# Attention into a SwiGLU feed-forward on one core: a wait ahead of later q loads, a last tile in three pieces, and a sum of squares as six products

## The chip, the cores and the metric

The kernel runs on one core of one Trainium2 chip. The metric is the device time of one execution in microseconds (us). Beside the times there is one profiled execution, taken by the hardware profiler, from which all views of the profile come. The names of the engines in the profile: PE is TensorE (its matmuls), PEld the weight loads of TensorE, which overlap PE, DVE is VectorE, ACT is ScalarE, POOL is GpSimd, SP is SyncE. An engine's name with a q behind it (SPq, POOLq) stands for its sequencer, which issues DMAs and waits on semaphores.

## The reference

Attention with a squared relu in the place of the softmax, and behind it an RMS norm and a feed-forward of SwiGLU form. The sizes are 8 batches, 12 heads, 448 positions, 64 columns to a head; 768 columns in the model, 1536 in the feed-forward.

```
scores = (1 / sqrt(64)) * (q @ k.T)             # per batch and head: 448 x 448
attn   = max(scores, 0) ** 2 / 448
x      = (attn @ v), heads side by side         # 3584 x 768
rms    = sqrt(mean(x * x, axis=-1) + 1e-6)
xn     = x / rms * rms_g
g      = xn @ w_gate                            # 768 -> 1536
val    = xn @ w_val
out    = (g * sigmoid(g) * val) @ w_out         # 1536 -> 768
```

All inputs and the output are float32; the kernel computes its products in bf16 with float32 accumulation.

## The kernel before

**Layout.** Everything is held transposed: x and xn have the model's columns on the partitions (6 blocks of 128) and the batch's 448 positions along the free axis; the hidden layer (hT) has 12 blocks of 128. A product with 128 rows of weights is split into two halves of the array, of 64 rows each (and, in the projections, 64 columns), which run beside each other: in the profile such a matmul is "64*64 64x448". Output tiles have 128 positions on the partitions; two batches (896 positions) make seven tiles. Tile 3 of each pair crosses the border of its batches.

**One batch's work.** q, k and v come from memory with a cast to bf16. Scores for two heads at a time (`scores_full`, L462) go to PSUM, from there through a relu into an r tile (L450, on ACT or DVE) and are squared in place (L454). `attend` (L562) multiplies them with v and evicts x to SBUF (L625). Then x's squares are summed: L635 squares in float32, L637 accumulates over pairs of blocks, `close` (L641) adds the last two, and a product with a matrix of ones (`norm_sums`, L856) sums over the partitions and spreads the result. `norm_scale` (L663) makes rstd by Ln and Exp on ACT and scales x to xn on DVE (L678). The feed-forward (`ffn`, L978) then has 24 projection groups, gate and value in turns (silu at L870, hidden product at L884), and, for each output tile, an out-projection (`outproj`, L911) in two groups of 384 columns with 24 half-array products each. `store` (L933) copies a group from PSUM to an output tile in SBUF (L941 on ACT, L939 on DVE); when both halves are there, `send` (L954) issues the tile's DMAs on SP (L964), one for each run of rows that lie together in memory.

**Batch 0 and the head.** Batch 0 is done in two halves of 224 positions so that the first products can start early. For its first half the squares are in bf16 (L629), and class `Sums` (L832) sums them with ones-products of the full array, two blocks at a time (L848). The second half is summed as every other batch is. Batches 0 and 1 are loaded in large pieces and transposed on PE (PE_T is 2). While the planner sees PE idle for more than 0.3 us in the head, it writes matmuls whose result nobody reads (`fill`, L1051) into the order.

**Later batches' loads.** Batches 2 to 7 are loaded in another form, with heads and columns side by side: q in one DMA of 112 x 4 x 768 elements, k in seven (L300), v in two (L286), all issued by POOL. SP then issues eight DMA transposes (`transpose_dma`, L314, L324) for a batch, four for k and four for q, which turn the loaded pieces into the operands of the scores. A load of batch b+2 may start when the buffer of batch b has been read: for q and k when batch b has been turned, for v when its last attention products are done.

**What sets the order.** The pools keep no order of their own: the whole order is written at build time by a planner (class Planner, L62 to L164), a small simulation of the five engines. Every `Op` has a cost for each engine that may run it, things that it depends on (`deps`), a rank, and for scores and attention a `due` condition, which asks how far the feed-forward of an earlier batch has come (`past`, L990, on the notes ("gv", fraction) and ("o", fraction) that a group carries). The planner always takes the engine whose next step can begin first, and lets the op write its instructions. The order on the chip is then fixed for each engine's queue, and semaphores between them follow from the data. `Stream` (L697) holds the feed-forward's groups and, in steps, emits one product of one group on the upper half of the array and one of another on the lower (`Group.emit`, L796, L802: nearly all matmuls of the feed-forward carry this one line). A DMA's landing time in the plan is estimated by `arrives` (L245): a fixed time, and kilobytes by a rate, one DMA after another. The main loop (from L1073) adds the work of batch b+2 (loads, transposes, attention) together with the feed-forward of batch b.

## Time and profile before

| what | us |
|---|---|
| three runs | 454.03, 454.59, 456.85; median 454.59 |
| the profiled execution | 453.62 |
| its span in the profile | 451.9 |
| PE busy | 440.2 |
| DVE, ACT, POOL busy | 241.7, 268.8, 76.8 |
| POOL busy with the 42 issues of k pieces (L300) | 33.1 |
| mean clock of TensorE over the span | 0.993 of full |

The span is the time from the first to the last record; 1.7 us of the profiled execution lie around it. A group's line in the profile has its source line, engine, operation, the tiles written and read, the number of partitions and elements, a count, then busy time and mean, and last the idle time of the engine just ahead of it with what ended it ("<-issue": nothing that the profile shows). In a timeline each row begins with its start in us from the span's start and its length. A row of a table by windows has the stretch, its length, then for PE, PEld, DVE, ACT and POOL the busy time with the number of instructions in brackets, then the mean clock that TensorE was granted, the share of the DMA engines (it passes 1 where packets overlap) and GB/s. In the clock's row of the page each digit is a fortieth of the span in tenths of full speed.

### The profile page before, as it was taken

The page shows a single profiled execution, that of the slowest core. Times are in us where ns is not written, and L with a number is a line of the kernel's source. Part 1 is how long each engine was busy: PE and PEld are TensorE (multiplying, and loading weights), DVE is VectorE, ACT ScalarE, POOL GpSimd, SP SyncE. Part 2 cuts the span into 40 slices and gives each one's busy share as a digit, 9 for nine tenths or more (in the row PEclk, how much of TensorE's full clock was granted, in tenths as well). Part 3 has the DMA queues.
Part 4 walks back from the last instruction along what each step waited for, and adds up shares of the span by engine and source line. Part 5 has one row for each costly group of instructions (what it writes and reads, how often), then busy time and mean ns, then how long its engine had stood idle before and what let it go on. Part 6 is the DMA issues. An engine that isn't in the chain of part 4 may idle for free.

```text
span 451.9 us, 16996 instructions
## 1 busy us (share of the span) xinstructions
PE 440.2 (97%) x7805; PEld 327.5 (72%) x7805; DVE 241.7 (53%) x403; ACT 268.8 (59%) x395; POOL 76.8 (17%) x96
## 2 busy tenths in 40 slices
PE   8899999998899999999999999999999999999995
PEld 6578777876568877677779765678778765787784
DVE  2867886566455456465655356566655356432200
ACT  2676986596447666587657657487657656342221
POOL 8522711472043000700043000100000000000000
PEclk9999999999899999999999999999999999999998
DMA  9999999999979921999039930980002200030013
GB/s 116 200 204 200 205 180 147 156 195 141 133 61 178 147 89 14 130 193 91 3 41 169 145 108 6 134 142 24 3 1 71 73 4 3 1 106 3 3 43 99
DMA packets 130039, 44.75 MB, mean 99 GB/s; under 512 B 102192, under 2 KB 126384, under 8 KB 129968
## 3 DMA queue, kind: packets, MB, share of 16 engines
q0 software_dynamic: 90912, 24.39, 58.5%
q1 hardware_dynamic: 39056, 19.28, 24.9%
q8 instruction: 61, 1.00, 1.0%
q14 instruction: 10, 0.08, 0.1%
HBM read 48.76 MB, written 11.01 MB: 132 GB/s over the span
## 4 chain that ended last, share of the span: by engine, by line
PE 88%; DMA 9%; issue 1%; POOL 1%; ACT 0%; ACTq 0%; POOLq 0%
PE psP L802 74%; PE psS L590 6%; PE psS L468 6%; DMA kb<-in_k_dram 4%; DMA wv_sb<-in_moe_w_val_dram 4%; DMA wo_sb<-in_k_dram 2%; PE psS L504 1%; PE psP L411 1%; POOL qb L286 0%; POOL wo_sb L270 0%; ACT ost L941 0%; POOL ident masks.py:199 0%; POOL ident masks.py:197 0%; ACTq L941 0%; POOLq L1126 0%
## 5 line engine op out<-in xcount | busy, mean ns | idle before, releaser
L802 PE MATMUL psP<-xn,wg_sb 64*64 64x448 bf16 (+1 forms) x2304 | 222.1, 340 | 0.0
L802 PE MATMUL psP<-xn,wv_sb 64*64 64x448 bf16 (+1 forms) x2304 | 204.6, 340 | 3.1 <-issue 3.1
L450 ACT ACTIVATE r<-psS 128x896 bf16<-128x896 f32 (+1 forms) x169 | 148.3, 913 | 47.3 <-PE psS L468 25.3
L802 PEld LDWEIGHTS <-wg_sb 64*64 64x64 bf16 (+1 forms) x2304 | 123.5, 105 | 39.8 <-PE psP L802 9.1
L454 DVE TENSOR_TENSOR r<-r 128x896 bf16<-128x896 bf16 (+1 forms) x171 | 102.9, 615 | 73.4 <-ACT r L450 72.8
L802 PE MATMUL psP<-wo_sb,hT 64*128 64x384 bf16 (+1 forms) x1502 | 139.5, 323 | 0.0
L802 PEld LDWEIGHTS <-wv_sb 64*64 64x64 bf16 (+1 forms) x2304 | 118.0, 105 | 29.0 <-issue 4.3
L802 PEld LDWEIGHTS <-hT 64*128 64x128 bf16 (+1 forms) x1502 | 101.8, 97 | 22.7 <-issue 2.8
L884 DVE TENSOR_TENSOR hT<-sil,psP 128x448 bf16<-128x448 bf16 (+1 forms) x108 | 61.1, 567 | 65.6 <-PE psP L802 50.3
L870 ACT ACTIVATE sil<-psP 128x448 bf16<-128x448 f32 (+1 forms) x108 | 55.1, 511 | 65.1 <-PE psP L802 54.7
L941 ACT COPY ost<-psP 128x384 f32<-128x384 f32 x55 | 26.3, 480 | 43.6 <-PE psP L802 42.4
L468 PE MATMUL psS<-qkT 64*64 64x448 bf16 (+1 forms) x412 | 50.5, 352 | 0.0
L590 PE MATMUL psS<-r,vb 64*64 64x448 bf16 (+1 forms) x756 | 45.8, 331 | 0.1
L678 DVE SCALAR_TENSOR_TENSOR xn<-xT,g_sb,rstd 128x448 bf16<-128x448 bf16 (+1 forms) x54 | 30.2, 629 | 21.9 <-ACT rstd L673 21.9
L286 POOL DMA_DIRECT2D vb<-in_v_dram x20 | 14.3, 724 | 160.6 <-PE psP L802 117.2
L300 POOL DMA_DIRECT2D kb<-in_k_dram x42 | 33.1, 1001 | 18.5 <-DMA wo_sb<-in_moe_w_out_dram 8.4
L625 ACT ACTIVATE xT<-psS 128x896 bf16<-128x896 f32 (+1 forms) x27 | 22.5, 833 | 18.2 <-PE psS L590 18.2
L590 PEld LDWEIGHTS <-vb 64*64 64x64 bf16 x756 | 24.5, 106 | 10.0 <-issue 1.8
L468 PEld LDWEIGHTS <-qkT 64*64 64x64 bf16 (+1 forms) x412 | 21.7, 104 | 5.9
L374 ACT ACT_TABLE_LOAD x18 | 23.1, 1283 | 1.0 <-PEq L1126 0.7
L635 DVE TENSOR_TENSOR x<-xT 128x896 f32<-128x896 bf16 (+1 forms) x16 | 16.5, 1031 | 9.9 <-ACT xT L625 9.9
L637 DVE TENSOR_TENSOR acc<-acc,x 128x896 f32<-128x896 f32 (+1 forms) x16 | 16.5, 1033 | 0.6
(41 smaller groups left out, 138.2 us busy)
## 6 DMA issues: line engine op xcount, KB each, us to landing
vb<-in_v_dram POOLq DMA_DIRECT2D x12, 384.0 KB, 7.7
qb<-in_q_dram POOLq DMA_DIRECT2D x6, 672.0 KB, 15.6
kb<-in_k_dram POOLq DMA_DIRECT2D x42, 96.0 KB, 14.2
out_dram<-ost SPq DMA_DIRECT2D x8, 336.0 KB, 4.6
wg_sb<-in_moe_w_gate_dram POOLq DMA_DIRECT2D x4, 576.0 KB, 16.8
wv_sb<-in_moe_w_val_dram POOLq DMA_DIRECT2D x4, 576.0 KB, 18.3
wo_sb<-in_moe_w_out_dram POOLq DMA_DIRECT2D x2, 1152.0 KB, 14.1
out_dram<-ost SPq DMA_DIRECT2D x8, 288.0 KB, 3.3
```

The lines of the kernel that those rows point to most:

```text
L300: nc.gpsimd.dma_start(out=to[:, u - u0 : u - u0 + step, h0:h1, :], in_=rows[:, u : u + step])
L374: nc.scalar.add_instruction(mybir.InstLoadActFuncSet(name=name, act_func_set_id=n, ins=[], outs=[]))
L450: nc.scalar.activation(out=op.view, in_=src, func=ACT.Relu)
L454: eng.tensor_tensor(out=rl.view, in0=rl.view, in1=rl.view, op=ALU.mult)
L468: nc.tensor.matmul(out=ps[m0:m1, hh, :S], lhsT=qkT[b][prt, j, 0, c * P + m0 : c * P + m1], rhs=qkT[b][prt, j, 1, :], start=True, stop=True,)
L590: mm = nc.tensor.matmul(out=ps[hh * D : (hh + 1) * D, jj, :w], lhsT=vb[prt, 2 * (j + jj) + hh, u * D : (u + 1) * D], rhs=r[prt, hh, :], st ...
L625: nc.scalar.mul(out=xTs[b][:, j : j + 2, lo : lo + w], in_=me.ps.tile[:, :, :w], mul=inv_attn)
L678: nc.vector.scalar_tensor_tensor(out=xns[b][:, kt, lo : lo + w], in0=xTs[b][:, kt, lo : lo + w], scalar=g_sb[:, kt : kt + 1], in1=rstd[:, ...
L802: mm = nc.tensor.matmul(out=self.ps[m0:m1, : self.w], lhsT=self.lhsT(i)[prt, m0:m1], rhs=self.rhs(i)[prt], start=(half == 0 and i == 0), s ...
L870: nc.scalar.activation(out=s[:, :w], in_=g.ps[:, :w], func=ACT.Silu)
L884: nc.vector.tensor_tensor(out=hT[:, fb, o : o + w], in0=sil[b, fb, lo][1][:, :w], in1=g.ps[:, :w], op=ALU.mult,)
L941: nc.scalar.copy(out=to, in_=g.ps[:, :w])
```

## The change

1. A q load of batch b+2, for b from 1, also waits for one feed-forward product of batch b. This product, the anchor, is the last product written in the first step whose group carries a note ("gv", at least 0.04), which is the second projection block of that batch. The wait is a dependence between the DMA's instruction on POOL and the matmul on PE. In the order that results, POOL's queue has for each of these batches: the seven k pieces, the first half of v, the q load, the second half of v. Before, it had both halves of v, q, then k. On SP, the four k transposes come ahead of the four q transposes for all batches from 3 on.
2. The planner's figures for DMAs are others (2.7 for the fixed time, rates of 300, 345 and 405 for some head loads, 1500 KB for the first gate slice), and every DMA of POOL is planned to start no earlier than the landing of the eighth before it. This concerns the plan alone. In the order that results, `fill` writes 110 matmuls of 128x224 instead of 97, and the transposes of batch 1 stand somewhat later among the products.
3. The sums of the second half of batch 0 are done as those of the first: three bf16 squares on DVE and six products of 128x224 on the full array (class `Sums`, now with the half and its parts as arguments), in the place of float32 squares, accumulation, `close` and two half-array products. The squares are written to the half's columns of batch 1's xn tile. In the second half, the r squares of its first two thirds may be planned on POOL; three of them are, between loads of batch 1. The planner's preference for ACT over DVE in the relu of batch 0's second half falls from 3.0 to 1.5, which moves one relu.
4. The last output tile is done in groups of 384, 192 and 192 columns. Each is sent as soon as it is copied: the first run of rows (16) on SP, the second (112) on ACT's queue. The two groups of 192 have 48 half-array products of 192 columns in the place of 24 of 384.

Counted in the two programs: PE 15,612 instructions before and 15,694 after, ACT 397 and 400, POOL 101 and 104, SP 107 and 108.

```diff
--- before.py
+++ after.py
@@ -244,12 +244,19 @@
         def ends(t):
-            dma_free[0] = max(dma_free[0], t + 2.4) + kb / rate
+            dma_free[0] = max(dma_free[0], t + 2.7) + kb / rate
             return dma_free[0] + 0.2
...
+    anchors = {}
     def pool_dma(cost, kb, rate, start, deps=()):
-        return add(Op({"POOL": cost}, lambda op: start(), deps, ends=arrives(kb, rate)))
+        deps = list(deps) + queue[-8:-7]
+        queue.append(add(Op({"POOL": cost}, lambda op: start(), deps, ends=arrives(kb, rate))))
+        return queue[-1]
+    queue = []
@@ -271,7 +278,7 @@
-            ops = [pool_dma(0.7, D * U * D * 4 * (h1 - h0) / 1e3, 400.0, runs_of_seven, deps)]
+            ops = [pool_dma(0.7, D * U * D * 4 * (h1 - h0) / 1e3, 300.0, runs_of_seven, deps)]
             landed.setdefault((nm, b), {}).update({h: ops for h in range(h0, h1)})
@@ -289,7 +296,7 @@
             if runs:
-                ops.append(pool_dma(0.72, kb, 400.0, whole, deps))
+                ops.append(pool_dma(0.72, kb, (300.0 if nm == 'q' else 345.0) if b == 0 else 400.0, whole, deps))
                 continue
@@ -297,9 +304,11 @@
                     rows = src.rearrange("h (p u) d -> p u h d", p=n)
-                    nc.gpsimd.dma_start(
+                    dma = nc.gpsimd.dma_start(
                         out=to[:, u - u0 : u - u0 + step, h0:h1, :], in_=rows[:, u : u + step]
                     )
+                    if step > 1 and b - 2 in anchors:
+                        tc.add_manual_dep(dma.ins, anchors[b - 2].ins.name, behind)
@@ -337,7 +346,7 @@
         dst, src = {"g": (wg_sb, moe_w_gate), "v": (wv_sb, moe_w_val)}[which]
-        w_in[which, s] = pool_dma(0.83, 1180, 400.0, lambda: nc.gpsimd.dma_start(
+        w_in[which, s] = pool_dma(0.83, 1180 if s or which == "v" else 1500, 405.0, lambda: nc.gpsimd.dma_start(
             out=dst[:, :, s * FS : (s + 1) * FS],
@@ -454,8 +463,10 @@
         rl = add(Op({"ACT": 0.05 + n * 0.833e-3, "DVE": 0.07 + n * 1.042e-3}, relu,
-                    [t] + r_ring.before, rank=2, lean={"DVE": 0.5 if key[:2] == (0, 0) else 3.0 if key[0] == 0 else 0.9}))
+                    [t] + r_ring.before, rank=2, lean={"DVE": 0.5 if key[:2] == (0, 0) else 1.5 if key[0] == 0 else 0.9}))
         on = {"DVE": 0.06 + n * 0.53e-3}
+        if key[:2] == (0, HS) and group[2] < HP - 2:
+            on["POOL"] = 0.05 + n * 1.82e-3
         sq = add(Op(on, square, [rl], rank=3))
@@ -605,13 +616,13 @@
             plan.take(op.ps.banks, [ev])
-            if (b, lo) == (0, 0):
+            if b == 0:
                 sq = add(Op({"DVE": 0.06 + 2 * w * 0.53e-3}, square_bf, [ev], rank=0))
-                squared[j] = sq
+                squared[lo, j] = sq
             else:
...
                 sq = add(Op({"DVE": cost}, square, [ev], rank=2))
-            if j == HP - 2 and (b, lo) == (0, 0):
+            if j == HP - 2 and b == 0:
                 summed[b, lo] = sq
@@ -626,7 +637,7 @@
             x = xTs[b][:, j : j + 2, lo : lo + w]
-            nc.vector.tensor_tensor(out=x2_bf[:, j : j + 2, :], in0=x, in1=x, op=ALU.mult)
+            nc.vector.tensor_tensor(out=xn_of[1][:, j : j + 2, lo : lo + w], in0=x, in1=x, op=ALU.mult)
@@ -655,7 +666,6 @@
     summed, squared, used = {}, {}, []
-    x2_bf = xn_of[1][:, :, :HS]
@@ -757,8 +767,12 @@
                 follow.finish(t)
-            if pair[0][1].note is not None:
-                state["phase"] = pair[0][1].note
+            note = pair[0][1].note
+            if note is not None:
+                state["phase"] = note
+                if note[1] == "gv" and note[2] >= 0.04 and note[0] not in anchors:
+                    anchors[note[0]] = mark = Done()
+                    mark.done, mark.ins = t + took + 0.3, pair[0][1].mm
             return took
@@ -832,25 +846,28 @@
-        def __init__(self):
-            before = []
-            for j in range(0, HP, 2):
-                deps = [Later(squared, j)] + before
-                before = [add(Op({"PE": 2 * HS / 2400.0}, self.products(j), deps, rank=-2, bank=j == 0, form="f"))]
+        def __init__(self, lo, parts):
+            self.lo, before = lo, []
+            for part in parts:
+                deps = [Later(squared, (lo, j)) for j in part] + before
+                cost = 2 * len(part) * (HS / 2400.0 + 0.0025)
+                fn = self.products([i for j in part for i in (j, j + 1)])
+                before = [add(Op({"PE": cost}, fn, deps, rank=-2, bank=part is parts[0], form="f"))]
             self.end = before[0]
-        def products(self, j):
+        def products(self, blocks):
             def fn(op):
-                if j == 0:
+                if blocks[0] == 0:
                     self.space, self.ps = op.ps, op.ps.tile
                     plan.take(op.ps.banks, [self.end])
-                for i in (j, j + 1):
+                for i in blocks:
                     nc.tensor.matmul(
-                        out=self.ps[:, :HS], lhsT=ones_bf[:], rhs=x2_bf[:, i, :],
+                        out=self.ps[:, :HS], lhsT=ones_bf[:],
+                        rhs=xn_of[1][:, i, self.lo : self.lo + HS],
                         start=(i == 0), stop=(i == KT - 1),
                     )
-                if j == HP - 2:
-                    norm_scale(0, 0, HS, self)
+                if blocks[-1] == KT - 1:
+                    norm_scale(0, self.lo, HS, self)
             return fn
@@ -906,6 +923,7 @@
     OW = DM // 2
+    LAST = (B // 2 - 1, NT - 1)
     osts, sent = {}, {}
@@ -920,17 +938,19 @@
-        for o in range(0, DM, OW):
+        for o, w in ((0, OW), (OW, OW // 2), (OW + OW // 2, OW // 2)) if (i, t) == LAST else ((0, OW), (OW, OW)):
             Piece(
-                trio, t in (0, S // P), FT, OW, lambda fk: hT[:, fk, t * P : (t + 1) * P],
-                lambda fk, o=o: wo_sb[:, fk, o : o + OW],
-                lambda g, o=o: store(i, t, o, OW, g), "psO", needs, False, note,
+                trio, t in (0, S // P), FT, w, lambda fk: hT[:, fk, t * P : (t + 1) * P],
+                lambda fk, o=o, w=w: wo_sb[:, fk, o : o + w],
+                lambda g, o=o, w=w: store(i, t, o, w, g), "psO", needs, False, note,
             )
...
     def store(i, t, o, w, g):
+        by_piece = (i, t) == LAST
         def fn(op):
@@ -940,32 +960,39 @@
             osts[i, t][1].append(op)
-            if len(osts[i, t][1]) == DM // w:
-                send(i, t)
+            osts[i, t][2] += w
+            if by_piece:
+                send(i, t, o, w, [op])
+            elif osts[i, t][2] == DM:
+                send(i, t, 0, DM, osts[i, t][1])
...
         if first:
-            osts[i, t] = [None, []]
-        op = add(Op({"ACT": 0.05 + w * 0.833e-3, "DVE": 0.07 + w * 1.042e-3}, fn, [g.end] + ([] if first else [osts[i, t][2]]),
+            osts[i, t] = [None, [], 0, None]
+        before = [] if first else [osts[i, t][3]]
+        op = add(Op({"ACT": 0.05 + w * 0.833e-3, "DVE": 0.07 + w * 1.042e-3}, fn, [g.end] + before,
                     rank=0, ring=ost_ring if first else None, lean={"DVE": 0.6}))
-        osts[i, t][2:] = [op]
+        osts[i, t][3] = op
         plan.take(g.space.banks, [op])
-    def send(i, t):
-        ost, copies, _ = osts[i, t]
+    def send(i, t, o, w, copies):
+        ost = osts[i, t][0]
         s, end = t * P, (t + 1) * P
...
             rows = out[b * S : (b + 1) * S, :].rearrange("(p u) m -> p u m", u=NCH)
+            on = "ACT" if (i, t) == LAST and m else "SP"
             def fn(op, n=n, c=c, p0=p0, s=s, rows=rows):
-                nc.sync.dma_start(
-                    out=rows[p0 : p0 + n, c, :], in_=ost[s - t * P : s - t * P + n, :]
+                eng = nc.scalar if op.engine == "ACT" else nc.sync
+                eng.dma_start(
+                    out=rows[p0 : p0 + n, c, o : o + w],
+                    in_=ost[s - t * P : s - t * P + n, o : o + w],
                 )
-            sent[i, t, m] = add(Op({"SP": 0.06}, fn, copies, ends=lambda t: t + 3.5))
+            sent[i, t, m] = add(Op({on: 0.06}, fn, copies, ends=lambda t: t + 3.5))
             s += n
@@ -1071,7 +1098,7 @@
     attention_half(0)
-    first = Sums()
+    first = Sums(0, [(0,), (2,), (4,)])
     for b in range(B):
@@ -1081,7 +1108,8 @@
             stream.add(groups[24:])
-            sums = [norm_sums(0, HS, HS), norm_sums(1, 0, S)]
+            Sums(HS, [(0, 2, 4)])
+            sums = [norm_sums(1, 0, S)]
         else:
@@ -1091,7 +1119,7 @@
                 seen = list(turned[b])
-            load("q", b + 2, deps=seen)
+            load("q", b + 2, deps=seen + ([Later(anchors, b)] if b else []))
             load("k", b + 2, deps=seen)
```

## The prediction

> **What bounds the kernel now.** I read the head of the page first, then the clock row and the chain of waits, then the gaps of PE one by one.
>
> ```profile
> span 451.9 us, 16996 instructions
> PE 440.2 (97%) x7805; PEld 327.5 (72%) x7805; DVE 241.7 (53%) x403; ACT 268.8 (59%) x395; POOL 76.8 (17%) x96
> ...
> PEclk9999999999899999999999999999999999999998
> ...
> q8 instruction: 61, 1.00, 1.0%
> ...
> PE 88%; DMA 9%; issue 1%; POOL 1%; ACT 0%; ACTq 0%; POOLq 0%
> ```
>
> PE is busy for 97% and makes 88% of the chain; the 9% of DMA are loads in the first 47 us. So a change of DVE, ACT or load work is paid only if it closes one of PE's few gaps, shortens the head, or shortens what follows the last matmul. Between the head and the tail the gaps are these, from PE's timeline (start, length, work, idle before):
>
> ```profile
> 105.46 0.35 PE L802 MATMUL psP<-xn,wv_sb 64*64 64x448 bf16 x1 [0.36 <-issue]
> ...
> 112.48 0.72 PE L802 MATMUL psP<-xn,wv_sb 64*64 64x448 bf16 x9 [0.77 <-issue]
> ...
> 120.87 0.39 PE L802 MATMUL psP<-xn,wv_sb 64*64 64x448 bf16 x1 [1.71 <-issue]
> ...
> 121.49 0.58 PE L802 MATMUL psP<-xn,wg_sb 64*64 64x448 bf16 x1
> ...
> 209.88 0.38 PE L802 MATMUL psP<-xn,wv_sb 64*64 64x448 bf16 x2 [0.28 <-issue]
> ```
>
> "issue" means that no semaphore held PE. Matmuls of 0.35 us take 0.58 after the third gap, because the clock fell. Two-microsecond windows (PE, PEld, DVE, ACT, POOL busy, clock, DMA share, GB/s) show the fall, and ten-microsecond ones the demand:
>
> ```profile
> 118.00:120.00 2.00, 1.16 (x19) 0.49 (x18) 1.69 (x3) 0.85 (x2) 0.00 (x0) 1.00 1.97 81
> 120.00:122.00 2.00, 1.13 (x16) 0.94 (x19) 0.00 (x0) 0.28 (x1) 0.00 (x0) 0.76 2.58 129
> 122.00:124.00 2.00, 2.00 (x27) 1.11 (x23) 0.00 (x0) 1.08 (x2) 0.00 (x0) 0.50 3.78 131
> 124.00:126.00 2.00, 2.00 (x43) 1.91 (x44) 1.16 (x2) 0.39 (x1) 0.00 (x0) 0.88 2.26 94
> ```
> ```profile
> 130.00:140.00 10.00, 10.00 (x147) 6.97 (x137) 4.50 (x7) 5.86 (x9) 9.03 (x10) 1.00 1.39 128
> ...
> 150.00:160.00 10.00, 10.00 (x212) 8.01 (x207) 4.90 (x8) 6.59 (x10) 0.00 (x0) 1.00 1.11 166
> ```
>
> My reading, an inference: PE runs out of instructions. The page has 61 instruction packets for 16,996 instructions, some 280 each. In projections PE consumes 212 + 207 in 10 us, a packet in 6.7 us; in out-projections 147 + 137, one in 10 us. Around 100 to 122 us, loads and DMA transposes overlap, and a packet that queues behind them comes late:
>
> ```profile
> 82.92 2.28 POOL L300 DMA_DIRECT2D qb<-in_q_dram  x1 [12.08 <-DMA qkT<-qb]
> ...
> 97.09 2.33 POOL L300 DMA_DIRECT2D qb<-in_q_dram  x1
> ```
> ```profile
> 94.84 8.22 SPq L324 DMA_TRANSPOSE qkT<-qb  x4
> ...
> 104.47 9.70 SPq L324 DMA_TRANSPOSE qkT<-kb  x4
> ```
>
> The q load of batch 3 is issued at 82.9 and lands in 11.9 us; that of batch 4 follows at 97.1 and takes 24.9, to 122. Price of these stalls: idle time in excess of flowing matmuls 0.66 + 1.07 + 2.01 (the printed 0.36, 0.77, 1.71 plus 0.3 each, since ends are modelled: the last matmul before a gap shows 0.35, while in the flow of 212 in 10 us one holds the array 0.05), at 209 us 0.59, and the clock 2·0.24 + 2·0.50 + 2·0.12 = 1.7. Sum 6.0 us: the most that the middle can give.
>
> [...] The gaps without a semaphore are in the rows, so I keep the 6.0 as a ceiling. [...]
>
> **The change, part by part.**
>
> *Loads (the wait).* The q load of batches 3 to 7 now waits for batch b-2's second projection block; its place on POOL moves behind the seven k pieces and the first half of v. Nothing is removed: 5 q issues of 2.3 us on POOL and all bytes stay. Queued behind the waiting issue on POOL are the second half of v and the next batch's k pieces; attention of that batch and SP's q transposes wait for those. On SP the k transposes now come ahead of the q ones, and for later batches three output transfers ahead of the q ones. By PE's order the wait ends at about 94 us for batch 3 (issued at 82.9 before), 151 for 4 (97.1), 203, 257 and 306 for 5, 6, 7 (132.0, 185.4, 233.9). So the load of batch 4 leaves the crowd at 97 to 122; batch 3's enters it. From each anchor to the first scores that need the q are 32 to 36 us for batch 3, more by 7 to 10 for the later ones. Needed: landing 12 to 25, four turns issued in 4.5 to 8.2, the last turn's landing 4.7 to 11.1: 22 to 44. In the middle, 30, it fits, and PE waits for nothing. Against that, q loads 4 to 7 leave out-projections (a packet in 10 us) for projections (one in 6.7).
>
> What remains of 6.0: the crowd of 94 to 121 still has one q load, its four turns and two batches' k and v, so I keep 2.8 of its 5.4; the 0.6 at 209, and about 0.2 of new gaps in projections, stay: 3.6. Gain 2.4. Ends: 6.0 gained if no gap is left, and 0 if each only moves; a loss is the slow rival below.
>
> *Sums of the second half as full products.* PE: six ones-products of 128x224 in the place of two half-array ones of the same width. At 0.093 us each (the flow of the fills, which are the same shape) against 0.047: 6·0.093 - 2·0.047 = +0.47. DVE loses two accumulations, their fp32 squares and a close, and gains three bf16 squares; before, rows of 128x448 show 0.62 each for both of the former. Some 1 us of DVE goes, but DVE is 53% busy and in front of PE only for the last square. Three r squares may go to POOL, which idles 2.2 us between loads of batch 1 ("[2.24 <-DMA wg_sb<-in_moe_w_gate_dram]" in its timeline). No row shows such a square on POOL; bounded by DVE's 0.39 and by POOL's longest issue, 2.3, it overruns its cover by at most 0.1 each. I take 0, end +0.3.
>
> *Planner's figures in the head.* Fills (matmuls that write nothing used) rise from 97 to 110: 13·0.093 = 1.2 us, most of it where PE would wait for a load; batch 1's transposes come later in order, with about 0.7 us more useful work ahead of the wait at 46.8 us for the last k piece. The head's loads keep their order and number, and the chain holds them to 46.6. DVE's shorter order takes 1 us from 14 to 22 us, which hardly reaches past that wait. Net with the sums' +0.47: -0.3; ends -1.3 (the 0.7 and 1.0 mostly paid) and +1.0 (the fills and sums uncovered, 1.7, less 0.7).
>
> *Tail.* The last matmuls, copy, issue and landing follow each other:
>
> ```profile
> 446.78 0.48 ACT L941 COPY ost<-psP 128x384 f32<-128x384 f32 x1 [1.48 <-PE psP L802]
> ```
> ```profile
> SPq L1137 <- DMA out_dram<-ost: 2.4, 1, 2.4
> ```
>
> The copy of 192 columns costs 0.16 less (0.833 ns a column, by the slope of the evictions). SP issues the last two parts at 447.28 and 447.64; with the longer part on ACT's queue beside SP, 0.36 goes. The final transfer, 336 KB in 2.9 us, becomes 84 KB; a 144 KB one shows 2.4 and a 96 KB one 1.8. I take 2.45, -0.45. PE: 24 products of 384 become 48 of 192, the same columns; the 24 weight loads added are hidden as long as one (0.097) passes beside 0.081 of product, so 0 to +0.3; I take +0.15. No row has a DMA issue on ACT: between SP's 0.32 and POOL's 0.72, 0 to +0.4 against SP; taken 0. Sum -0.97 + 0.15 = -0.8, ends -1.3 and -0.2.
>
> **Sum**, on the profiled execution of 453.62 us (451.9 span and 1.7 around it): -2.4 - 0.8 - 0.3 = 450.1. The median shown, 454.59, stands 0.97 above it: **451.1 us**, 0.8% faster. A step of 1%, 4.5 us, is about the smallest that a measurement of this kernel tells from no change.
>
> **Rivals.**
> 1. *The whole of the stalls goes.* For: the longest gap ends as the q load of batch 4 lands, at 122, and that load is moved by 54 us. Against: half the crowd stays. 454.59 - 6.0 - 0.8 - 0.3 = 447.5.
> 2. *The change moves the stalls and no more* (or they aren't of the loads' making). For: the same bytes and turns, and loads put in the phase with the quicker consumption. Against: only one gap past 122 in spite of four later loads. Tail and head remain: 454.59 - 1.1 = 453.5.
> 3. *Slower: the wait takes the place of the gaps.* PE waits at batch 3's first scores, at about 129 us, for a q load started 11 us later than before and in the crowd. With landing 24.9 (as for batch 4), turns 8.2 and 11.1 for the last, 44.2 are needed where 35 are there: 9.2, and 1.7 of clock. 454.59 - 3.5 + 10.9 = 462.0. It decides once the landing is beyond about 16 us with slow turns; at 20 us, 4.3 late plus 1.7 makes 454.59 - 3.5 + 6.0 = 457.1. Against: before, with q and k loads nearly alone, 11.9 to 12.1 are the rule.
>
> **How the numbers follow.** Forecast 451.1 with 0.46, first rival 0.21, second 0.20, third 0.13. The range takes in the first rival with the better ends of head and tail (447.5 - 1.0 = 446.5) and the third's milder half (457.5): 446.5 to 457.5 leaves 0.1 above and little below, and the spread of small terms takes the rest. Faster by over 1% (below 450.0): the first rival and a third of the forecast's spread (448.5 to 453.5), 0.38. Slower by over 1%: most of the third, and new stalls in projections, 0.15. Within 1%: 0.47.
>
> **What would show it.** Fewer "issue" gaps at 95 to 125 us, clock 1.00 at 122; POOL's q rows near 94, 151, 203, 257, 306, released by PE; no PE gap at 129 to 134 released by a transpose; PE's last copy to the end in about 4.1 us where it was 5.1 with a copy of 192 columns; six L848-type products more. Wrong would make it: PE gaps released by "qkT" (third rival), "issue" gaps within 150 to 180 us (second), or a head that ends later than 47 us.

## The result and the profile after

The changed kernel is slower by little: 456.82 us in the median of 13 runs (455.32 to 458.08) against 454.03 for the kernel before in as many (451.89 to 456.85). The ratio is 1.0057, with a 95% interval of 1.0036 to 1.0078. The profiled execution took 457.69 us, with a span of 455.9.

From the page of the changed kernel, the lines that answer to those of before (span, PE, clock, instruction packets, chain):

```profile
span 455.9 us, 17092 instructions
...
PE 442.7 (97%) x7846; PEld 328.2 (72%) x7846; DVE 243.2 (53%) x398; ACT 268.4 (59%) x395; POOL 81.1 (18%) x99
...
PEclk9999999999899999999999999999999999999999
...
q8 instruction: 61, 1.00, 1.0%
...
PE 93%; DVE 2%; DMA 2%; issue 2%; ACT 0%; POOL 0%; POOLq 0%
```

Three shares of the chain moved: DMA fell from 9% to 2%, DVE came in with 2%, and "issue" doubled. The first two belong together: on the way back through the head the chain now goes over DVE, and not over loads. To place the differences I took five marks from the traces: the start of the first silu, of the first output copy (82.60 us before), of the 37th silu (155.11, batch 3), of the last tile's first copy (444.82), and the end of the span. The stretches between them, in us:

| kernel | to first silu | to first output copy | to silu 37 | to last tile's first copy | to the end |
|---|---|---|---|---|---|
| before | 30.22 | 52.38 | 72.51 | 289.71 | 7.04 |
| changed | 33.12 | 52.89 | 73.40 | 291.14 | 5.34 |
| difference | +2.90 | +0.51 | +0.89 | +1.43 | -1.70 |

So the head lost 3.4, the middle 2.3, and the tail won 1.7; the sum is 4.03, the difference of the two spans (the medians differ by 2.8). This is where the prediction went wrong, and each stretch has its lines.

**Head.** PE's timeline of the changed kernel, 26 to 42 us, has two waits for DVE; before, it had no idle time in this window:

```profile
29.68 0.27 PE L816 MATMUL psP<-xn,wv_sb 64*128 64x224 bf16 x2 [0.89 <-DVE xn L688]
31.31 0.25 PE L816 MATMUL psP<-xn,wv_sb 64*128 64x224 bf16 x1 [1.36 <-DVE xn L688]
```

The six xn blocks that PE waits for take 4.96 us where the kernel before has 2.26. From DVE's timeline, before and changed, and from POOL's in the changed kernel (start, length):

```profile
26.09 2.26 DVE L678 SCALAR_TENSOR_TENSOR xn<-xT,g_sb,rstd 128x224 bf16<-128x224 bf16 x6 [1.35 <-ACT rstd L673]
```
```profile
26.66 4.96 DVE L688 SCALAR_TENSOR_TENSOR xn<-xT,g_sb,rstd 128x224 bf16<-128x224 bf16 x6 [1.35 <-ACT rstd L683]
```
```profile
27.52 1.86 POOL L463 TENSOR_TENSOR r<-r 128x896 bf16<-128x896 bf16 x1 [2.74 <-ACT r L459]
29.32 0.71 POOL L293 DMA_DIRECT2D kb<-in_k_dram  x1
30.05 0.95 POOL L463 TENSOR_TENSOR r<-r 128x448 bf16<-128x448 bf16 x1
...
34.65 1.68 POOL L463 TENSOR_TENSOR r<-r 128x896 bf16<-128x896 bf16 x1 [3.01 <-ACT r L459]
```

In the window of 28 to 32 us PE is busy for 1.75 of 4.00 us, and DVE throughout; first the changed kernel, then the one before:

```profile
28.00:32.00 4.00, 1.75 (x30) 1.21 (x27) 4.00 (x4) 2.77 (x4) 3.62 (x4) 1.00 1.32 203
```
```profile
28.00:32.00 4.00, 4.00 (x67) 3.31 (x71) 3.27 (x8) 3.97 (x7) 0.66 (x1) 1.00 1.32 203
```

Row by row, four blocks take 0.44 to 0.45 us and two 1.87 (from 27.75) and 1.71 (from 29.55). Both overlap a square on POOL. A DVE square of r, 0.61 to 0.63 us elsewhere in this stretch, takes 1.97 beside the third one (from 34.84). The square that goes to POOL costs POOL nothing; it costs DVE. From the start of the first xn block to the first silu are 6.46 us in the changed kernel and 4.13 before: of the 2.90 us, 2.33 lie behind that start.

**Middle.** One long stop stands in the place of three, and two new ones come later, all "issue":

```profile
118.00 0.35 PE L816 MATMUL psP<-xn,wv_sb 64*64 64x448 bf16 x1 [4.22 <-issue]
...
177.83 0.35 PE L816 MATMUL psP<-xn,wv_sb 64*64 64x448 bf16 x1 [0.90 <-issue]
...
227.40 0.38 PE L816 MATMUL psP<-xn,wv_sb 64*64 64x448 bf16 x4 [0.49 <-issue]
```

The two-microsecond windows (PE, PEld, DVE, ACT, POOL busy, clock, DMA share, GB/s) show PE empty for four microseconds while DVE and ACT still finish their work, and the clock at 0.61 and 0.54 after it:

```profile
114.00:116.00 2.00, 0.00 (x0) 0.00 (x0) 1.78 (x3) 0.68 (x2) 0.00 (x0) 1.00 3.04 131
116.00:118.00 2.00, 0.00 (x0) 0.00 (x0) 0.49 (x1) 0.00 (x0) 0.00 (x0) 1.00 1.06 65
118.00:120.00 2.00, 2.00 (x28) 1.38 (x31) 0.00 (x0) 0.92 (x1) 0.75 (x1) 0.61 2.74 148
120.00:122.00 2.00, 2.00 (x32) 1.30 (x27) 1.16 (x2) 0.07 (x1) 0.00 (x0) 0.54 3.33 143
```

**Tail.** The last copy, and the issue of the longer part on ACT's queue, from the timeline:

```profile
452.56 0.32 ACT L961 COPY ost<-psP 128x192 f32<-128x192 f32 x1 [0.74 <-PE psP L816]
452.91 0.38 ACTq L990 DMA_DIRECT2D out_dram<-ost  x1
```

From the start of the last copy to the end are 3.33 us; before, 5.08.

### The profile page after: what moved, and what is told of

The parts are those of the page before. It is cut to its first block, busy times and chain, and to the rows that moved or that the text cites. A ratio compares the mean times of both kernels' runs of the same rounds, so it can differ in the third digit from the quotient of the medians.

```text
span 455.9 us, 17092 instructions
## 1 busy us (share of the span) xinstructions
PE 442.7 (97%) x7846; PEld 328.2 (72%) x7846; DVE 243.2 (53%) x398; ACT 268.4 (59%) x395; POOL 81.1 (18%) x99
## 4 chain that ended last, share of the span: by engine, by line
PE 93%; DVE 2%; DMA 2%; issue 2%; ACT 0%; POOL 0%; POOLq 0%
PE psP L816 77%; PE psS L601 7%; PE psS L479 6%; DMA wo_sb<-in_k_dram 2%; DVE xn L688 1%; PE psS L515 1%; PE psP L420 1%; DVE r L463 1%; PE psP L1078 1%; PE psS L497 0%; PE psP L864 0%; POOL qb L293 0%; DVE qkT L430 0%; PE psP L412 0%; DVE r L457 0%
## 5 line engine op out<-in xcount | busy, mean ns | idle before, releaser
L816 PE MATMUL psP<-wo_sb,hT 64*128 64x384 bf16 (+2 forms) x1526 | 139.5, 321 | 0.0
L816 PEld LDWEIGHTS <-wv_sb 64*64 64x64 bf16 (+1 forms) x2304 | 116.8, 105 | 30.9 <-issue 5.4
L961 ACT COPY ost<-psP 128x384 f32<-128x384 f32 (+1 forms) x56 | 26.4, 474 | 44.1 <-PE psP L816 43.7
L479 PE MATMUL psS<-qkT 64*64 64x448 bf16 (+1 forms) x412 | 51.6, 353 | 0.0
L688 DVE SCALAR_TENSOR_TENSOR xn<-xT,g_sb,rstd 128x448 bf16<-128x448 bf16 (+1 forms) x54 | 32.9, 676 | 22.7 <-ACT rstd L683 22.7
L293 POOL DMA_DIRECT2D vb<-in_v_dram x20 | 15.8, 797 | 84.6 <-PE psP L816 53.6
L307 POOL DMA_DIRECT2D qb<-in_q_dram x6 | 13.7, 2277 | 79.4 <-PE psP L816 77.7
L646 DVE TENSOR_TENSOR x<-xT 128x896 f32<-128x896 bf16 x14 | 15.2, 1089 | 6.7 <-ACT xT L636 6.7
```

Source lines behind the costliest of these rows:

```text
L307: dma = nc.gpsimd.dma_start(out=to[:, u - u0 : u - u0 + step, h0:h1, :], in_=rows[:, u : u + step])
L479: nc.tensor.matmul(out=ps[m0:m1, hh, :S], lhsT=qkT[b][prt, j, 0, c * P + m0 : c * P + m1], rhs=qkT[b][prt, j, 1, :], start=True, stop=True,)
L688: nc.vector.scalar_tensor_tensor(out=xns[b][:, kt, lo : lo + w], in0=xTs[b][:, kt, lo : lo + w], scalar=g_sb[:, kt : kt + 1], in1=rstd[:, ...
L816: mm = nc.tensor.matmul(out=self.ps[m0:m1, : self.w], lhsT=self.lhsT(i)[prt, m0:m1], rhs=self.rhs(i)[prt], start=(half == 0 and i == 0), s ...
L961: nc.scalar.copy(out=to, in_=g.ps[:, :w])
```

## The experiments

The theory after these readings: POOL's squares hold DVE (head), and PE stops where the next block of instructions is late (middle). Rivals: the planner's other order makes the head long; the wait itself makes the stops in the middle. All ratios are to the kernel before, with the runs of the same chip. Two kernels, e5 and e10, leave work out: they fill three r tiles with zeros instead of squaring them. The stretches of each profile, as in the table above:

| run | to first silu | to first output copy | to silu 37 | to last tile's first copy | to the end | median | ratio (interval) |
|---|---|---|---|---|---|---|---|
| e1 | 30.96 | 52.89 | 70.13 | 290.75 | 5.34 | 451.95 | 0.9954 (0.9925 to 0.9984) |
| e2 | 33.44 | 52.89 | 71.82 | 289.05 | 5.33 | 453.59 | 0.9997 (0.9968 to 1.0027) |
| e3 | 30.54 | 52.36 | 73.92 | 289.24 | 5.34 | 452.65 | 0.9957 (0.9924 to 0.9990) |
| e4 | 31.50 | 52.36 | 69.48 | 289.06 | 6.96 | 452.09 | 0.9959 (0.9931 to 0.9987) |
| e5 | 31.09 | 52.89 | 71.16 | 290.13 | 5.33 | 451.57 | 0.9964 (0.9940 to 0.9988) |
| e6 | 30.50 | 53.68 | 70.91 | 289.32 | 6.98 | 453.15 | 0.9991 (0.9968 to 1.0015) |
| e7 | 32.43 | 52.89 | 71.97 | 293.23 | 5.87 | 457.06 | 1.0077 (1.0044 to 1.0110) |
| e8 | 30.80 | 52.37 | 70.83 | 289.17 | 5.33 | 449.46 | 0.9906 (0.9878 to 0.9935) |
| e9 | 32.60 | 52.37 | 69.44 | 289.06 | 5.34 | 453.15 | 0.9973 (0.9936 to 1.0009) |
| e10 | 33.48 | 53.49 | 71.77 | 290.27 | 5.35 | 456.05 | 1.0045 (1.0013 to 1.0078) |
| e11 | 31.53 | 53.74 | 69.11 | 289.17 | 5.34 | 451.81 | 0.9936 (0.9907 to 0.9965) |
| e12 | 30.46 | 52.37 | 69.92 | 289.28 | 5.33 | 449.43 | 0.9923 (0.9894 to 0.9952) |

Between kernels with the same order in it, the second stretch repeats within 0.02 us, and the last (but for e7) within 0.1; the first varies by 1.3 (30.22 to 31.53 in the kernels with the old figures and no hold), and the third by 1.4 (72.51 and 73.92 in before and e3, whose orders are equal there). Part of the variation is the clock: in e4 and e11, the two highest in the first stretch, it was granted at 0.50 for 3.4 us from 15 to 19 us. A difference in the first or third of under 1.5 us in one profile therefore tells nothing by itself. Steadier for the head is the time from the start of the first xn block to the first silu: 4.13 us in each of the nine kernels in which nothing holds DVE up, 6.46 in the three with POOL's squares (changed, e2 and e7).

### e1: the changed kernel without POOL's squares

```diff
-        if key[:2] == (0, HS) and group[2] < HP - 2:
-            on["POOL"] = 0.05 + n * 1.82e-3
```

> The changed kernel, but the three r squares of batch 0's second half that stood on POOL are planned on DVE again; nothing else of the source differs. Theory 1 (a DVE instruction that reads two SBUF operands stands still while POOL squares): no DVE xn row of 1.7 to 1.9 us is left at 27 to 31 us, all are near 0.44; the first silu begins at 30.4 to 31.0 us instead of 33.1, the loss of 3.4 us at the end of the head shrinks to 0.5 to 1.2, and the ratio to the kernel before falls from 1.0057 to about 1.000 to 1.002. Rival (the planner's later transposes and added fills make the head long): the first silu stays beyond 32 us and the ratio within 0.002 of 1.0057.

The first silu comes at 30.96, and the time falls by 4.9 us, from 456.82 to 451.95 (4.7 by the ratios), twice what the theory asked for. The xn blocks take 0.44 to 0.45 us each, and 2.3 us of the gain lie between the first of them and the first silu. The profiles show 3.3 us more in the third stretch (70.13 instead of 73.40), which varies by 1.4. The added fills and later transposes as the cause of the long head are out: they are still there.

### e2: the changed kernel without the wait

```diff
-                    if step > 1 and b - 2 in anchors:
-                        tc.add_manual_dep(dma.ins, anchors[b - 2].ins.name, behind)
...
-            load("q", b + 2, deps=seen + ([Later(anchors, b)] if b else []))
+            load("q", b + 2, deps=seen)
```

> The changed kernel without the wait of the q loads for a feed-forward product, in the plan and on the chip; POOL squares, sums, tail and the planner's figures stay. Theory A (the wait itself makes the losses in the middle): the issue gaps of 4.2 us at 114 to 118, 0.9 at 177.8 and 0.5 at 227.4 go, gaps of 0.3 to 1.8 as in the kernel before come back, and about 2.3 us are gained: ratio about 1.001. Theory B (PE runs out of instructions wherever a fetched block meets a crowd of DMA packets, and the wait only moves the meeting): gaps with no releaser of 1 to 4 us appear at other places, the ratio lies anywhere between 1.000 and 1.010, and no gap ends on a q transpose. The head is unchanged in both, first silu near 33.1.

This is as theory A has it in size: three gaps of 1.2, 1.6 and 1.0 us at 109, 117 and 125, none at 178 or 227, and 453.59. Theory B's range takes it in too. In the changed kernel the wait costs some 3 us. That it does so by itself is denied by e4.

### e3: only the tail

The functions `outproj`, `store` and `send` of the changed kernel, all else as before; its core:

```diff
-        for o in range(0, DM, OW):
+        for o, w in ((0, OW), (OW, OW // 2), (OW + OW // 2, OW // 2)) if (i, t) == LAST else ((0, OW), (OW, OW)):
...
+            on = "ACT" if (i, t) == LAST and m else "SP"
```

> The kernel before with only the last tile's groups of 384, 192 and 192 columns, each sent by itself on two queues. The profiles of the two kernels differ by 1.69 us between the first copies of the last tile and the end. If that is the tail's own worth: ratio 0.9963, the trace equal to that of before up to 440 us in every milestone within 0.1 us apart from the gaps without releaser, last copy of 0.32 us. By the prediction's own step it would be 0.8 us: ratio 0.998. If the difference came from the DMA engines' load alone and not from the pieces: 1.000.

The last stretch is 5.34, as in the changed kernel: the tail is worth 1.70 us, and the ratio agrees (0.9957).

### e4: only the wait

The anchor in `Stream.step` and the lines that e2 took out, put into the kernel before; in its plan both halves of v stay ahead of q.

```diff
+                if note[1] == "gv" and note[2] >= 0.04 and note[0] not in anchors:
+                    anchors[note[0]] = mark = Done()
+                    mark.done, mark.ins = t + took + 0.3, pair[0][1].mm
...
+                    if step > 1 and b - 2 in anchors:
+                        tc.add_manual_dep(dma.ins, anchors[b - 2].ins.name, behind)
...
-            load("q", b + 2, deps=seen)
+            load("q", b + 2, deps=seen + ([Later(anchors, b)] if b else []))
```

> The kernel before with only the wait of the q loads of batches 3 to 7 (plan and chip); in this plan both halves of v still go ahead of q on POOL. Theory A (the wait makes the middle worse by itself): q issued near 94 us for batch 3, gaps without releaser in all above 5 us, ratio 1.005. Theory B (only the meeting of blocks and crowds moves): ratio between 0.990 and 1.010, by the sum of the gaps that the profile shows, which should account for the change of the profiled time within 0.5 us. Third theory of the prediction (a wait for q transposes at batch 3's first scores): a PE gap released by a transpose between 125 and 136 us, over 3 us long, ratio above 1.008.

Theory A had the sign wrong, and theory B had left it open: 0.9959. Alone, the wait pays 1.8 us by the medians, and the third stretch is 69.48 instead of 72.51. From the table of waits, the row of PE with no releaser, before and here (total, times, longest):

```profile
PE psP L802 <- issue: 3.1, 4, 1.7
```
```profile
PE psP L810 <- issue: 1.6, 2, 1.3
```

No gap ends on a q transpose: the rival in which the wait takes the place of the stops didn't occur.

### e5: POOL fills instead of squaring

```diff
-            eng.tensor_tensor(out=rl.view, in0=rl.view, in1=rl.view, op=ALU.mult)
+            if op.engine == "POOL":
+                eng.memset(rl.view, 0.0)
+            else:
+                eng.tensor_tensor(out=rl.view, in0=rl.view, in1=rl.view, op=ALU.mult)
```

> The changed kernel in which the three squares on POOL are left out and POOL fills the same r tiles with zeros instead (so these scores count as zero); every engine's order is the same, instruction for instruction. Theory (DVE stood still because POOL read SBUF through what they share): a fill reads nothing, so DVE's xn rows stay near 0.44 us, the first silu begins at 30.4 to 31.3 us, the head is 1.8 to 2.4 us shorter than in the changed kernel, ratio to the kernel before about 1.001 plus or minus 0.003 by the gaps in the middle. Rival 1 (any POOL instruction on SBUF holds DVE up): xn rows of 0.8 us or more remain, first silu beyond 31.5. Rival 2 (the order of the head makes it long): first silu at 33.1 as in the changed kernel.

DVE and POOL of this kernel, from their timelines:

```profile
26.96 2.26 DVE L691 SCALAR_TENSOR_TENSOR xn<-xT,g_sb,rstd 128x224 bf16<-128x224 bf16 x6 [1.34 <-ACT rstd L686]
```
```profile
27.79 0.85 POOL L464 MEMSET r<- 128x896 bf16 x1 [3.50 <-ACT r L459]
```

A POOL instruction that reads nothing stands beside the fourth xn block, and the six blocks take 2.26 again. The order is the changed kernel's to the instruction, so the order isn't the cause; POOL's square is. What a fill leaves out of it is the reading and the product. The time is 451.57 us, 5.2 less than with the squares (4.2 by the ratios).

### e6: only the sums

Class `Sums` of the changed kernel with its bf16 squares, in the kernel before, without squares on POOL.

```diff
-            if (b, lo) == (0, 0):
+            if b == 0:
                 sq = add(Op({"DVE": 0.06 + 2 * w * 0.53e-3}, square_bf, [ev], rank=0))
...
-            sums = [norm_sums(0, HS, HS), norm_sums(1, 0, S)]
+            Sums(HS, [(0, 2, 4)])
+            sums = [norm_sums(1, 0, S)]
```

> The kernel before with only the sums of the second half as six ones-products (three bf16 squares on DVE, no squares on POOL, old figures in the plan, no wait, old tail). By the prediction's step: +0.47 of PE time less what DVE's shorter work brings, so milestones after 60 us within -0.5 to +0.5 us of the kernel before, apart from the gaps at block boundaries; ratio 0.997 to 1.003. Rival (the sums make the head longer by over 0.5 us): all milestones from 60 to 100 us later by 0.7 or more than the first one at 30 us.

The second stretch grows from 52.38 to 53.68: the sums cost 1.3 us, not 0.5 at most, so the rival of this run is right for the head. The total shows no cost: 0.9991, with an interval of 0.9968 to 1.0015.

### e7: the changed kernel with fills of double width

```diff
-        for _ in range(int((t1 - t0 - 0.15) / 0.1)):
-            nc.tensor.matmul(out=s.tile[:, :HS], lhsT=ones_bf[:], rhs=busy_bf[:, :HS], start=True, stop=True)
+        n = int((t1 - t0 - 0.15) / 0.1)
+        for w in [S] * (n // 2) + [HS] * (n % 2):
+            nc.tensor.matmul(out=s.tile[:, :w], lhsT=ones_bf[:], rhs=busy_bf[:, :w], start=True, stop=True)
```

> The changed kernel, in which two fills of 128x224 are one of 128x448, so that 54 matmuls and 54 weight loads go from the head with no array time (110 fills become 56). Theory B (PE waits for the next 256 instructions): every gap without releaser stands at a matmul whose number in PE's order is 92 above a multiple of 128, as all gaps so far (1628, 1756, 1884, 2012, 2140; a few less beyond 2900), which is 54 matmuls later in the work than in the changed kernel, about 2.6 us; PE goes on 1.2 to 1.9 us after the last instruction packet has ended; the size of the gaps changes, the head does not (within 0.4 us). Rival (PE's operands or the crowd itself stop it): the 4.2 us gap stands before the same product as in the changed kernel, number 1884 - 54 = 1830.

The gaps between 95 and 130 us, from PE's timeline:

```profile
110.62 0.95 PE L816 MATMUL psP<-xn,wv_sb 64*64 64x448 bf16 x16 [0.95 <-issue]
...
118.73 0.35 PE L816 MATMUL psP<-xn,wv_sb 64*64 64x448 bf16 x1 [1.81 <-issue]
...
126.57 0.35 PE L816 MATMUL psP<-xn,wg_sb 64*64 64x448 bf16 x1 [1.13 <-issue]
```

Counted in the order of PE's matmuls, with the end of the last instruction packet (queue q8) before each:

```
kernel    gap ends  matmul  less 92, by 128   packet ended   PE goes on after
before     105.46    1756        13               103.99           1.47
before     112.48    1884        14               111.14           1.34
before     120.87    2012        15               118.47           2.40
changed    118.00    1884        14               116.52           1.49
e7         110.62    1756        13               109.14           1.47
e7         118.73    1884        14               117.19           1.55
e7         126.57    2012        15               125.15           1.42
```

Each gap of this stretch, in every kernel, stands at the same place of a grid of 128 matmuls with their 128 weight loads, 256 instructions. The packets of q8 have 16,384 bytes each, and their 61 times 256 are 15,616 instructions, against PE's 15,612 in the kernel before. In e7 that is a product 54 matmuls further on in the work: the gaps stay with the count and leave the products. That settles what they are: PE waits for its next instructions. The first silu at 32.43 was a little more than 0.4 from 33.12, within that stretch's variation; from the first xn block it is 6.46 us, as in the changed kernel.

### e8: the wait and the tail

The diffs of e3 and e4 together, on the kernel before.

> The kernel before with the wait of the q loads and the last tile in three pieces, and nothing else of the change. If both parts add up as measured alone (0.9959 and 0.9957, the profiles -3.7 us in the middle and -1.7 at the end): ratio 0.990 to 0.994, about 450. If the wait's gain was luck of the meeting of blocks and loads that does not come again although PE's order up to the last tile is the same: 0.995 to 0.998.

The parts add up: 449.46 in six runs, ratio 0.9906, 4.5 us under the kernel before on the same chip and some 7 under the changed one (7.4 by the medians, 6.9 by the ratios). This version beats both.

### e9 and e10: DVE held without squares

Into e8 (as e9) and into e5 (as e10):

```diff
             def fn(op):
+                if (b, lo) == (0, 0) and kt in (3, 4):
+                    nc.vector.memset(x2[:], 0.0)
+                    nc.vector.memset(x2[:, 0, :], 0.0)
                 xns[b] = xn_of[b % 2]
```

> The kernel of the run before with wait and tail on the kernel before, in which DVE is held in the head: two fills of an unused float32 tile, of 128x896 and 128x448, ahead of each of the blocks 3 and 4 of xn of the first half, about 2.6 us of DVE time in all, where POOL's squares held it in the changed kernel. PE's order is unchanged, instruction for instruction. Theory S (the loads of the head keep to their own time, so a head that is 2 us late makes the blocks of instructions and the crowd of loads at 95 to 122 us meet in another way, and this costs the changed kernel its extra 2.7 us in the middle): first silu about 2.2 us later, and another 1.5 to 4 us lost between 95 and 235 us; ratio to the kernel before 0.998 to 1.004. Rival (the delay costs itself alone): milestones behind 240 us later by 2.0 to 2.6 us; ratio 0.995 to 0.997.

> The changed kernel with POOL's three squares left out for fills with zeros, as in e5, and DVE held by the same four fills as in e9, where the squares held it. All that differs from the changed kernel is who holds DVE; PE's order is the same. Theory S: the time of the changed kernel comes back, 456 to 458, ratio 1.004 to 1.009, with a gap or gaps of 4 us or more in all between 95 and 235 us. Rival: e5's time plus the 2.0 to 2.6 us that the head is later, ratio 1.000 to 1.003.

DVE of e10, from its timeline:

```profile
27.52 0.81 DVE L691 MEMSET x<- 128x896 f32 x1
28.48 0.43 DVE L692 MEMSET x<- 128x448 f32 x1 [0.16 <-DVE x L691]
28.83 0.33 DVE L694 SCALAR_TENSOR_TENSOR xn<-xT,g_sb,rstd 128x224 bf16<-128x224 bf16 x1
29.30 0.81 DVE L691 MEMSET x<- 128x896 f32 x1
30.26 0.43 DVE L692 MEMSET x<- 128x448 f32 x1 [0.16 <-DVE x L691]
```

With DVE held by fills of 0.81 and 0.43 us twice, e5 comes back to about the changed kernel: 456.05 against 451.57, and 456.82 for the changed one (ratios 1.0045, 0.9964, 1.0057). In e8 the ratio rises from 0.9906 to 0.9973. So holding DVE there is enough to cost 3.7 us (e10) and 3.0 (e9) by the ratios, without a square on POOL. From the first xn block to the first silu are 6.60 us in e9 and 7.27 in e10, instead of 4.13.

That a hold costs more than its delay, as theory S has it, isn't shown. e9's ratio lies between the ranges of S and the rival, and its interval reaches into both; its profile shows no loss behind the head (69.44 in the third stretch). e10's ratio is in S's range, but its interval reaches into the rival's, and its gaps from 95 to 235 us come to 4.2 us where e5 without the hold has 3.6. e10's profile shows another loss: the clock was granted at 0.50 from 31.8 to 35.3 us, right behind PE's waits for DVE. The clocks of all runs point there too. By an estimate, the share of the clock that wasn't granted times a run's time, the mean loss is 1.8 us in e9 and 1.9 in e10, 2.5 in the changed kernel, against 1.0 in e8, 0.7 in e5 and 1.3 in e1.

### e11: the plan's old figures, no squares

The changed kernel without POOL's squares and with `arrives` and the rates of the kernel before:

```diff
-            dma_free[0] = max(dma_free[0], t + 2.7) + kb / rate
+            dma_free[0] = max(dma_free[0], t + 2.4) + kb / rate
...
-        deps = list(deps) + queue[-8:-7]
```

> The changed kernel without POOL squares and with the plan's old figures for DMAs (no limit of eight, 97 fills): wait, sums and tail alone. If the figures are worth nothing in the head: first silu 30.3 to 31.0, milestones at 84 to 98 us later than in the kernel before by 1.0 to 1.5 us, as with the sums alone (1.4 to 1.6) and with the figures (1.25). If the figures pay for the sums, as the prediction had it: later by 2 us or more without them. Ratio 0.990 to 0.997, by the gaps.

The second stretch is 53.74, as with the sums alone (53.68); with the new figures it is 52.89 in all five kernels that have them and DVE unheld by fills. So the figures give back 0.8 of the 1.3 us that the sums cost. In the fourth stretch they lose it again: it has 289.1 to 289.3 us in all kernels with the wait and the old figures, 290.1 to 293.2 with the new ones and the wait, with gaps like those at 177.8 and 227.4. The medians of e11 and e1, which differ by the figures alone, are level (451.81 and 451.95).

### e12: k waits as well

e8, in which the first k piece of a batch from 4 on waits with its q:

```diff
-                    if step > 1 and b - 2 in anchors:
+                    if (step > 1 or (b > 3 and u == 0)) and b - 2 in anchors:
...
-            load("k", b + 2, deps=seen)
+            load("k", b + 2, deps=seen + ([Later(anchors, b)] if b > 1 else []))
```

> The kernel of e8 (wait and tail on the kernel before), in which from batch 4 on the first k piece of a batch waits for the same product as its q load, so that the seven k pieces of batch 4 leave the crowd of 97 to 122 us and come behind q of batch 4 at about 153. Theory (a packet of instructions is late by what lies in the DMA engines ahead of it): between 95 and 125 us the gaps at matmuls 1756, 1884 and 2012 come to less than 1 us in all (e8: 3.1, printed), and if nothing new comes at 153 to 182, where q and k of one batch now stand together, the middle gains 2 to 3 us on e8: ratio 0.984 to 0.989. Rival 1 (the crowd moves with its k pieces): gaps of 1 to 2 us at block boundaries between 155 and 185, 205 and 235: ratio 0.989 to 0.993 or above. Rival 2 (k of batch 4 comes too late): a PE gap released by a k transpose near 182 us, ratio above 0.995.

It is level with e8 by the medians (449.43), and its ratio, 0.9923, misses the theory's range; no gap came between 155 and 235 us, as rival 1 had it. At matmul 1884 a gap remains though batch 4's k isn't there:

```profile
113.78 0.72 PE L810 MATMUL psP<-xn,wv_sb 64*64 64x448 bf16 x9 [1.87 <-issue]
```

The two gaps left, 0.35 and 1.87, are less than e8's 3.1 but not under 1 us: k of batch 4 isn't needed to make this packet late. What makes it late stays open.

## Why the prediction was wrong

**The three r squares on POOL: "I take 0, end +0.3".** This step failed. I asked whether POOL had idle time for the squares, and it had; whom they disturb I didn't ask. Measured: 1.43 and 1.27 us more for two xn blocks on the path of the first products, 2.33 us from the first of these blocks to the first silu, and 4.9 us of the median with all that follows (e1; e5 says 5.2; by the ratios 4.7 and 4.2). e10 brings most of it back by holding DVE alone. That step by itself turns the forecast's gain into a loss: without the squares the change is a gain of 0.5% (e1, 0.9954), where 0.8% was forecast.

**Sums, +0.47, and the planner's figures, -0.3 net.** The figures were sized right: from +0.47 to -0.3 is -0.77, and they give back 0.8 in the head (e11). The sums were mis-sized: +1.3 in the head (e6). Together that is +0.5 instead of -0.3. What makes the sums dearer than their array time wasn't tried. What I missed is that the figures' order, together with the wait, later brings gaps of its own: 1.0 (e5), 1.6 (e1) and 2.0 us (the changed kernel) over the 289.1 to 289.3 of the fourth stretch.

**Loads, -2.4.** That PE stops for late instruction packets was right, shown by e7, though the 280 instructions to a packet should have been 256: the packets of q8 are PE's alone by their count. That the crowd of loads makes them late was argued and isn't shown: without batch 4's k a packet was as late (e12). The clock fell after the gap in the changed kernel (to 0.50 for 3.4 us, after 4.2 us of stop), as before (0.50 for 3.4, after 1.7); in e5 and e12 it stayed at 1.00 after stops of 2.1 and 1.9 us, so the 1.7 us of clock doesn't come with every such stop. q was issued at 96.8, 156.3, 206.9 where I expected 94, 151, 203, later by roughly what PE had lost by then. The wait's worth alone, -1.8 (e4), was near. In the changed kernel the stops grew instead of shrinking: there the wait costs some 3 us (e2), while in the kernel before it pays, and in the one with the new tail too (3.2 by the medians of e8 and e3, 2.3 by the ratios). These kernels differ in the squares, the sums and the figures; the changed kernel without both squares and wait wasn't run, so which of them turns the sign stays open.

**Tail, -0.8.** Right, and undersized: -1.70. The term that was off is the last transfer. Taken was 2.45 us; the DMA issues of the last six microseconds show it, with the group before it, as

```profile
out_dram<-ost ACTq DMA_DIRECT2D x2, 84.0 KB, 1.9
```

and the last of the two took 1.81 from its issue, where 336 KB took 2.86: -1.05 instead of -0.45. The 24 weight loads more cost PE 0.05, not 0.15: from the first to the last copy of the last tile are 2.01 us where there were 1.96.

**Rivals.** None of the three was this result. The slow one, a wait of PE for q's transposes, didn't come: batch 3's q took 21.3 us to land, beyond its point of decision of 16, yet its last turn landed at 130.4, and PE never waited for it. From the issue that is 33.6 us; the middle of my 22 to 44 was 33, not the 30 that I wrote. "The change moves the stalls and no more" described the middle of the changed kernel best, and its sign, a gap between 150 and 180 us, came at 177.8. The measured time lies 0.7 us inside the upper end of the range, which is luck: it got there by a way that was not among the cases. With the squares' +0.3 the head could lose 1.3 at most; it lost 3.4.

## What to carry to other kernels

Before work is moved to an idle engine, look at what its instruction does to the work that runs beside it: a square on POOL, itself off the path, quadrupled a DVE instruction on it (1.87 us instead of 0.44); a fill in its place didn't (e5, six blocks in 2.26). Where PE stops with no releaser, count its instructions: here the stops lay multiples of 256 apart, stayed with the count when 54 products went (e7), and ended 1.2 to 2.4 us after an instruction packet. Moving loads away from such a place was worth trying, but not sure: for q it paid (e4, 1.8 us by the medians), for k it didn't (e12, level with e8). And take a change of several parts to pieces: two of four here were worth 4.5 us, the other two took away some 7.

## What the runs showed of the hardware

- In the changed kernel two of DVE's xn blocks of 128x224 took 1.87 and 1.71 us beside POOL's squares, where the other four took 0.44 to 0.45, and a DVE square of 128x896 took 1.97 instead of 0.61 to 0.63. Beside POOL fills of the same r tiles (e5) the six blocks took 2.26 us together, as in the kernel before. So here POOL's squares held DVE up, and its fills, which read nothing, didn't. Through what a square holds DVE up no run shows. The second held row begins at 29.55, before the row of the square beside it (30.05).
- A POOL square of 128x896 took 1.68 and 1.86 us beside DVE, one of 128x448 0.95; DVE's own are 0.62 and 0.39.
- PE's stops of over 0.25 us behind the head, 1 to 6 in each of the 14 profiles, lie multiples of 256 instructions apart (from matmul 2779 on up to three matmuls short of it), last 0.3 to 4.2 us, and end 1.2 to 2.4 us after an instruction packet has ended. Of 61 packets, four ended in such a stop in the kernel before and three in the changed one.
- The share of the DMA engines doesn't tell where a stop comes: two-microsecond windows with one show 0.5 (changed, 176 to 178 us) to 3.0 (114 to 116), and one of 3.3 (changed, 120 to 122) has PE busy throughout.
- The clock fell to 0.50 after a stop of 4.2 us (changed), and in the kernel before to 0.50 after one of 1.7; it stayed at 1.00 after one of 2.1 (e5) and one of 1.9 (e12). A fall lasted 3.4 us in each of the five profiles that have one before the end.
